# Two halves of a rational feed-forward step told apart on VectorE, with empty instructions between them

## The chip, the core and the metric

The kernel runs on one core of a Trainium2 chip. What counts is the device time of one launch in microseconds: the median of several executions. A profiled execution of the same program gives the rows quoted below.

## What is computed

For each of four batches, q, k and v of 6080 tokens by 256 channels give a channel attention (256 x 256, softmax over the last axis); its output, 24320 tokens of 256, goes through a feed-forward step of width 2048 whose activation is a rational function. Cut to what matters:

```python
qn = q / (norm(q, axis=1) + 1e-6); kn = k / (norm(k, axis=1) + 1e-6)
a = softmax(kn.transpose(0, 2, 1) @ qn / tau)      # 256 x 256 for each batch
x = (v @ a).reshape(24320, 256)
h = x @ w_in                                       # 24320 x 2048
P = a0 + a1 * h + a2 * h**2 + a3 * h**3
Q = 1 + abs(b0) * abs(h) + abs(b1) * h**2
out = (P / (Q + 1e-6)) @ w_out                     # 24320 x 256
```

## The kernel before

**Tiling.** Tokens lie on the free axis in groups of 512 (twelve a batch, the last of 448; 48 in all); the 2048 hidden channels lie on the partitions in 16 blocks of 128, taken two at a time. A *pair* is one group and two such blocks: eight pairs a group, 384 in all. Attention and w_in are fused into weights w before (`fuse`), so a pair starts with v.

**One pair** (`pair`, line 894). Its hidden values sit in `hx`, a PSUM tile of two banks, one for each block or *half* x = 0, 1; there are three such tiles. The names used below: *mm1* (TensorE, 12 matmuls, hx from vhi, vlo and w), *abs*, *zz*, *shift*, *root* and *square* (ScalarE, into d, uu and r, each over both halves), *num* (VectorE, hx from uu and hx, both halves), *one* (GpSimd, d), *quot* (VectorE, gh from hx and r, both halves), *again* (GpSimd, d times gh, by halves). Then by halves on VectorE, lines 998 to 1003: *rest* (hx of the half, less d) and *last* (gl of the half from hx and r). gh and gl are the high and low parts of the result; TensorE multiplies them with w_out into acc (*out_hi*, *out_lo*, 12 matmuls a pair). In the trace: rest is `hx<-hx,fast,d`, last is `gl<-hx,r`, num is `hx<-uu,fast,hx`, quot is `gh<-hx,fast,r`.

**Other work on VectorE.** A group ends with a transpose of acc into orow, and each next group's v is transposed into orow; sums of the scores (sacc) and low parts of w are mixed in.

**Order.** A `Planner` (line 134) gives each engine a fixed order of steps from costs and due times written by hand (`LAG`, `TIME`). Each engine then issues its instructions in that order: `InOrder` (line 73) ties every instruction to the one before it on its engine, as an order without a wait. All instructions are recorded by its line 83, so the trace shows that line for all and one goes by tiles.

**Waits.** The framework finds dependences from the tiles that instructions touch and makes a semaphore wait of each, also between two instructions of one engine. An instruction holds one wait; a further one stands in a sequencer instruction ahead of it. `apart` (line 340) declares two instructions on different halves of one hx tile as independent, if they are on different engines and share no other buffer. `half[0]` (line 495) tells it which hx tile and bank the running step uses. Two half steps on the same engine stay dependent.

**Which branch.** `body(True)` and `body(False)` are two versions of the whole program, chosen on the chip by the coefficients; with these inputs the first runs.

Of the kernel before, what the change touches and what calls it, by code (L numbers as in the profile page):

```python
# [129 lines left out]
def flat(bufs):  # L130
    return [x for b in bufs for x in (b.both if isinstance(b, Pair) else [b])]
# [165 lines left out]
def tile_channel_attention_rational_ffn(  # L297
# [37 lines left out]
    FRONT = 10  # L335

    half = [None]
    seen = {}

    def apart(eng, ins):  # L340


        if half[0] is None:
            return
        slot, bank, rest = half[0]
        for other, old, used in seen.get((slot, 1 - bank), ()):
            if other is not eng and not used & rest:
                tc.declare_no_dep(ins.ins, old.ins, reason="the two use different banks of one tile")
        mine = seen.setdefault((slot, bank), [])
        mine.append((eng, ins, rest))  # L350
        del mine[:-40]

    pe = InOrder(tc, nc.tensor, apart)
    dve = InOrder(tc, nc.vector, apart)
    act = InOrder(tc, nc.scalar, apart)
    pool = InOrder(tc, nc.gpsimd)
    sp = InOrder(tc, nc.sync)
# [16 lines left out]
    def buf(tag, shape, dtype=F32, name=None):  # L374


        def view(slot):
            sizes = dict(zip("abc", shape[1:]))
            t = homes[tag][slot]
            if t.dtype != dtype:  # L380
                t = t.bitcast(dtype)
            t = t[:, : math.prod(shape[1:])]
            names = " ".join(sizes)
            return t.rearrange(f"p ({names}) -> p {names}", **sizes) if len(sizes) > 1 else t

        homes.setdefault(tag, 0)
        homes[tag] = max(homes[tag], math.prod(shape[1:]))
        return Buf(tag, view)
# [54 lines left out]
    c0, c1, c2, l3, l2, lam, half2, kappa, eps, gain, x, y, z = (fast[:, i : i + 1] for i in range(13))  # L443
# [29 lines left out]
    def body(quick):  # L473
# [1 line left out]
        plan = planner(when)  # L475
        first = []
        II, T0 = when["pair"], when["start"]
        def step(eng, cost, key, fn, reads=(), writes=(), port=False, rank=None, ahead=None):
            new = [b for b in flat(writes) if b.tag is not None and not b.writers]
            used = {id(b): b for b in (*flat(reads), *flat(writes))}.values()  # L480
            own = [b for b in used if b.tag in ("hA", "hB")]
            rest = [b for b in used if b.tag not in ("hA", "hB")]

            def run():
                for b in new:
                    b.tile = b.view(b.slot)
                if ahead is not None:
                    where = [(b.tag, b.slot) for b in new]
                    if ahead in sent:
                        assert sent[ahead] == where  # L490
                        return
                    sent[ahead] = where
                at = {(b.slot, b.tag == "hB") for b in own}
                if len(at) == 1:
                    half[0] = *at.pop(), {(b.tag, b.slot) if b.tag else id(b) for b in rest}
                fn()
                half[0] = None

            begun = plan.add(eng, cost, key, run, reads, writes, port, rank)
            if ahead is not None:  # L500
                first.append(begun)
# [4 lines left out]
        def piece(side, m, at, c):  # L506
# [72 lines left out]
            else:  # L579
                dst, ok = None, w_out_ok[m]  # L580
                where = slice(2 * m, 2 * m + 2)
                whi, wlo = (x[:, where].rearrange("p f e -> p (f e)") for x in (w_out_hi, w_out_lo))
            step("SP", 1.45, at, load, (), [raw])
            step("ACT", 0.67, c, rescale, [raw], [kept])
            one, two = (0.45, 0.7) if port else (0.62, 0.7)
            step("POOL", 0.6, c + 0.05, sign, [kept], [kept])
            step("DVE", two, c + 0.1, top_bits, [kept], [work], port)
            step("DVE", one, c + 0.2, power, [work], [work], port)
# [305 lines left out]
        def pair(m, at, vparts, w, acc):  # L894
# [3 lines left out]
            s = n / 512  # L898
            (vhi, vlo), (whi, wlo) = vparts, w
            hx = banks()  # L900
            d, r = buf("d", [P, 2, GT]), buf("r", [P, 2, GT])
            y = buf("uu", [P, 2, GT], F32, "uu")

            def c(b):
                return b[:, :, :n]

            def due(name):
                x = lag[name]
                return at + (x[p] if isinstance(x, tuple) else x)

            def mm1(i):
                idx = 0
                for e in range(NC2):
                    for a, x in ((whi, vhi), (whi, vlo), (wlo, vhi)):
                        pe.matmul(
                            hx[:, i, :n], a[:, e, i * P : (i + 1) * P], x[:, e, :n],
                            start=(idx == 0), stop=(idx == 3 * NC2 - 1),
                        )
                        idx += 1

            for i in range(2):
                fn = lambda i=i: mm1(i)
# [8 lines left out]
                                start=(first and i == parts[0] and a is w[0]), stop=(last and i == 1 and a is w[-1]),  # L931
                            )

            def put(eng, per, fixed, name, fn, reads, writes, rank=None, later=0.0):
                step(eng, per * s + fixed, due(name) + later, fn, reads, writes, False, None if rank is None else at + rank)

            if quick:
                fn = lambda: act.activation(c(d), c(hx), AF.Abs)
                put("ACT", 0.87, 0.16, "abs", fn, [hx], [d], 1.0)
                fn = lambda: act.activation(c(y), c(hx), AF.Square, bias=half2)  # L940
                put("ACT", 0.87, 0.25, "zz", fn, [hx], [y], 1.0)
                fn = lambda: act.activation(c(d), c(d), AF.Square, bias=1.0)
                put("ACT", 0.87, 0.2, "shift", fn, [d], [d])
                fn = lambda: dve.scalar_tensor_tensor(c(hx), c(y), kappa, c(hx), op0=ALU.add, op1=ALU.mult)
                put("DVE", 1.06, 0.23, "num", fn, [y, hx], [hx])
                fn = lambda: act.activation(c(r), c(d), AF.Abs_reciprocal_sqrt, bias=eps)
                put("ACT", 0.87, 0.3, "root", fn, [d], [r], 6.0)
                fn = lambda: pool.tensor_scalar(c(d), c(d), ones[:, 0:1], eps, op0=ALU.mult, op1=ALU.add)
                put("POOL", 1.06, 0.18, "one", fn, [d], [d])
                first = c0  # L950
            else:
                kk = buf("uu", [P, 2, GT], F32, "kk")
                fn = lambda: act.activation(c(kk), c(hx), AF.Abs, scale=b1)
                put("ACT", 0.87, 0.25, "kk", fn, [hx], [kk], 1.0)
                fn = lambda: dve.scalar_tensor_tensor(c(d), c(kk), b0, c(hx), op0=ALU.add, op1=ALU.mult)
                put("DVE", 1.06, 0.22, "prod", fn, [kk, hx], [d], 1.0)
                fn = lambda: act.activation(c(d), c(d), AF.Abs)
                put("ACT", 0.87, 0.2, "absd", fn, [d], [d])
                fn = lambda: act.activation(c(y), c(hx), AF.Identity, scale=a3, bias=a2)
                put("ACT", 0.87, 0.33, "slope", fn, [hx], [y], 1.0)  # L960
                fn = lambda: dve.tensor_tensor(c(y), c(y), c(hx), op=ALU.mult)
                put("DVE", 1.06, 0.16, "num1", fn, [y, hx], [y])
                fn = lambda: dve.scalar_tensor_tensor(c(hx), c(y), a1, c(hx), op0=ALU.add, op1=ALU.mult)
                put("DVE", 1.06, 0.23, "num2", fn, [y, hx], [hx])
                fn = lambda: act.activation(c(r), c(d), AF.Abs_reciprocal_sqrt, bias=ONE)
                put("ACT", 0.87, 0.2, "root", fn, [d], [r], 6.0)
                fn = lambda: pool.tensor_scalar(c(d), c(d), ones[:, 0:1], ONE, op0=ALU.mult, op1=ALU.add)
                put("POOL", 1.06, 0.07, "one", fn, [d], [d])
                first = a0
            fn = lambda: act.activation(c(r), c(r), AF.Square)  # L970
# [3 lines left out]
            ghi, glo = buf("gh", [P, 2, GT], F32R), buf("gl", [P, 2, GT], F32R)  # L974
            ghi_ok = Buf()
            t_ok, glo_ok = ([Buf() for _ in range(2)] for _ in range(2))
            fn = lambda: dve.scalar_tensor_tensor(c(ghi), c(hx), first, c(r), op0=ALU.add, op1=ALU.mult)
# [11 lines left out]
            if AGAIN == "whole":  # L989
                fn = lambda: pool.tensor_tensor(c(d), c(d), c(ghi).bitcast(F32), op=ALU.mult)  # L990
                put("POOL", 2.32, 0.1, "again", fn, [d, ghi, ghi_ok], t_ok)

            def tail(x):
                h = hx.both[x]
                if AGAIN != "whole":
                    fn = lambda: pool.tensor_tensor(d[:, x, :n], d[:, x, :n], ghi[:, x, :n].bitcast(F32), op=ALU.mult)
                    put("POOL", 1.16, 0.145, "again", fn, [d, ghi, ghi_ok], [t_ok[x]], later=0.1 * x)
                fn = lambda: dve.scalar_tensor_tensor(
                    hx[:, x, :n], hx[:, x, :n], first, d[:, x, :n], op0=ALU.add, op1=ALU.subtract
                )  # L1000
                put("DVE", 0.53, 0.23, "rest", fn, [h, d, t_ok[x]], [h], later=0.1 * x)
                fn = lambda: dve.tensor_tensor(glo[:, x, :n], hx[:, x, :n], r[:, x, :n], op=ALU.mult)
                put("DVE", 0.53, 0.155, "last", fn, [h, r, *([glo] if x else [])], [glo_ok[x], *([] if x else [glo])], 10.0, 0.1 * x)

            for x in range(2):
                tail(x)
                out_hi(x)
                out_lo(x)
# [67 lines left out]
        for G in range(TG):  # L1076
            b, g = divmod(G, NG)
            at = T0 + G * NFP * II
# [60 lines left out]
```

## Time and profile before

| | |
|---|---|
| median of 3 runs | 2483.2 us (2482.13 to 2484.92) |
| the profiled execution | 2482.81 us, its span 2481.4 us |
| TensorE busy (granted clock 0.986 on the mean) | 2377.6 us, 96% |
| VectorE busy | 2208.8 us, 89% |
| ScalarE busy | 2061.9 us, 83% |
| GpSimd busy | 1844.5 us, 74% |

Busy means that an instruction of the engine was under way; waits of the sequencers are not in it. In a timeline row the first number is the start, the second how long the instruction took (several, where it ends in x2), and the bracket how long the engine had stood idle before it and what ended that. Two rows of one engine give the time from start to start, and so whether the second began before the first had ended.

### The profile page before, as it was taken

Reading aid. Unit: us, or ns where it says so; the run is one execution under the profiler, and the core shown is the slowest. Engines: PE = TensorE matmul, PEld = TensorE weight load, DVE = VectorE, ACT = ScalarE, POOL = GpSimd, SP = SyncE. Lnnn points to the kernel's source line nnn. Section 1 sums busy time; section 2 is a strip of 40 time slices with the busy share of each in tenths; the row PEclk is TensorE's granted clock in tenths of the full one; section 3 lists DMA queues with packets and bytes.
Section 4 is the critical chain, followed back from the end, with each engine's and each line's share of the span. In section 5 each row is a group of like instructions: output and inputs, shape, how many; then the busy total and the mean of one; then the engine's idle time right before and its main releaser. Section 6 shows DMA issues by size and latency. Waiting matters only on the chain.

```text
span 2481.4 us, 30690 instructions
## 1 busy us (share of the span) xinstructions
PE 2377.6 (96%) x10312; PEld 1926.9 (78%) x10312; DVE 2208.8 (89%) x2645; ACT 2061.9 (83%) x2052; POOL 1844.5 (74%) x1424
## 2 busy tenths in 40 slices
PE   6599999999999999999999999999999999999998
PEld 5477777887788887777778888777777877777776
DVE  4779999979978889999997889999998999999997
ACT  4589999868777789899977778899996989999896
POOL 6798777787669977777767896777774777777775
PEclk9799999999999999999999999999999999999999
DMA  8433112271246731211225661211211121111201
GB/s 261 127 104 58 18 18 35 65 145 24 43 103 133 161 58 18 34 18 18 34 59 124 128 128 25 35 18 18 34 17 18 18 33 18 25 28 18 32 11 18
DMA packets 455864, 141.17 MB, mean 57 GB/s; under 512 B 395888, under 2 KB 445040, under 8 KB 455696
## 3 DMA queue, kind: packets, MB, share of 16 engines
q1 hardware_dynamic: 447152, 108.04, 20.9%
q0 software_dynamic: 8544, 31.07, 6.9%
q8 instruction: 83, 1.36, 0.2%
q14 instruction: 85, 0.70, 0.1%
HBM read 83.10 MB, written 24.90 MB: 44 GB/s over the span
## 4 chain that ended last, share of the span: by engine, by line
PE 58%; DVE 25%; issue 9%; ACT 3%; POOL 3%; DMA 2%; DVEq 0%; SPq 0%; POOLq 0%; ACTq 0%
PE hx L83 34%; PE acc L83 24%; DVE hx L83 10%; DVE gl L83 5%; DVE gh L83 5%; DVE orow L83 2%; POOL d L83 2%; ACT d L83 1%; ACT uu L83 1%; ACT r L83 1%; DMA d<-in_moe_w_in_dram 1%; POOL orow L83 0%; POOL uu L83 0%; DVEq L83 0%; DVE kq L83 0%
## 5 line engine op out<-in xcount | busy, mean ns | idle before, releaser
L83 POOL TENSOR_TENSOR d<-d,gh 128x512 f32<-128x512 f32 (+1 forms) x768 | 977.4, 1302 | 491.4 <-DVE gh L83 478.4
L83 PE MATMUL hx<-vhi,w 128*128 128x512 f32 (+1 forms) x3072 | 1055.9, 396 | 36.5 <-DVE gl L83 30.2
L83 PEld LDWEIGHTS hx<-vhi,w 128*128 128x128 f32 x3072 | 577.4, 188 | 224.7 <-DVE gl L83 104.7
L83 DVE SCALAR_TENSOR_TENSOR hx<-hx,fast,d 128x512 f32<-128x512 f32 (+1 forms) x768 | 574.7, 748 | 80.8 <-POOL d L83 51.0
L83 PE MATMUL hx<-vlo,w 128*128 128x512 f32 (+1 forms) x1536 | 597.8, 389 | 0.0
L83 ACT ACTIVATE uu<-hx,fast 128x1024 f32<-128x1024 f32 (+1 forms) x384 | 422.6, 1100 | 173.6 <-PE hx L83 169.9
L83 DVE TENSOR_TENSOR gl<-hx,r 128x512 fp32r<-128x512 f32 (+1 forms) x768 | 521.0, 680 | 40.2 <-PE acc L83 4.0
L83 DVE SCALAR_TENSOR_TENSOR hx<-uu,fast,hx 128x1024 f32<-128x1024 f32 (+1 forms) x384 | 487.1, 1268 | 36.2 <-ACT d L83 19.2
L83 POOL TENSOR_SCALAR d<-d,ones,fast 128x1024 f32<-128x1024 f32 (+1 forms) x384 | 467.9, 1218 | 68.8 <-ACT r L83 65.8
L83 DVE SCALAR_TENSOR_TENSOR gh<-hx,fast,r 128x1024 fp32r<-128x1024 f32 (+1 forms) x384 | 484.5, 1262 | 32.6 <-ACT r L83 26.8
L83 PE MATMUL acc<-gh,w_out_hi 128*128 128x512 f32 (+1 forms) x1536 | 476.9, 392 | 1.9 <-DVE sacc L83 0.9
L83 ACT ACTIVATE d<-hx 128x1024 f32<-128x1024 f32 (+1 forms) x384 | 387.6, 1009 | 109.0 <-PE hx L83 89.2
L83 PE MATMUL acc<-gl,w_out_hi 128*128 128x512 f32 (+1 forms) x1536 | 475.2, 391 | 2.7 <-DVE gl L83 2.4
L83 PE MATMUL acc<-gh,w_out_lo 128*128 128x512 f32 (+1 forms) x1536 | 472.0, 389 | 0.0
L83 ACT ACTIVATE r<-d,fast 128x1024 f32<-128x1024 f32 (+1 forms) x384 | 439.3, 1144 | 11.9
L83 ACT ACTIVATE r<-r 128x1024 f32<-128x1024 f32 (+1 forms) x384 | 403.2, 1050 | 8.9
L83 ACT ACTIVATE d<-d 128x1024 f32<-128x1024 f32 (+1 forms) x384 | 403.7, 1051 | 7.5
L83 PEld LDWEIGHTS acc<-gl,w_out_hi 128*128 128x128 f32 x1536 | 288.4, 188 | 62.5 <-DVE gl L83 5.5
L83 PEld LDWEIGHTS acc<-gh,w_out_hi 128*128 128x128 f32 x1536 | 288.9, 189 | 60.5 <-DVE orow L83 2.3
L83 PEld LDWEIGHTS acc<-gh,w_out_lo 128*128 128x128 f32 x1536 | 289.5, 189 | 58.0
L83 PEld LDWEIGHTS hx<-vlo,w 128*128 128x128 f32 x1536 | 289.3, 188 | 47.6
L83 PE MATMUL hx<-kq 128*128 128x256 f32 (+1 forms) x592 | 135.8, 384 | 8.3 <-DVE fast L83 7.5
(111 smaller groups left out, 1147.1 us busy)
## 6 DMA issues: line engine op xcount, KB each, us to landing
ssq<-sq POOLq DMA_DIRECT2D x54, 512.0 KB, 4.9
vst<-in_v_dram SPq DMA_DIRECT2D x176, 128.0 KB, 4.0
out_dram<-orow SPq DMA_DIRECT2D x176, 128.0 KB, 3.3
kq<-in_k_dram SPq DMA_DIRECT2D x78, 256.0 KB, 4.3
kq<-in_q_dram SPq DMA_DIRECT2D x78, 256.0 KB, 4.6
d<-in_moe_w_in_dram SPq DMA_DIRECT2D x8, 512.0 KB, 6.6
ssq<-sq POOLq DMA_DIRECT2D x6, 448.0 KB, 5.4
d<-in_moe_w_out_dram SPq DMA_DIRECT2D x4, 512.0 KB, 3.8
```

What stands on the lines that cost most here:

```text
L83: ins = op(*args, **kwargs)
```

## The change

`apart` gets a fourth entry, a *lane*: (pair, half) for the steps rest and last of the branch-independent tail, none for all others. Two instructions whose lanes name the same pair and different halves are now declared independent also on the same engine, and without the test for shared buffers. Where a step with a lane comes right behind a step of the same engine with the same pair and the other half, an empty instruction (`dve.nop()`) is issued between the two; it goes through `InOrder` as well, so the order runs through it. The planner's input is the same.

```diff
@@ -335,19 +335,20 @@
     FRONT = 10
 
     half = [None]
-    seen = {}
+    seen, recent = {}, {}
 
     def apart(eng, ins):
 
 
         if half[0] is None:
             return
-        slot, bank, rest = half[0]
-        for other, old, used in seen.get((slot, 1 - bank), ()):
-            if other is not eng and not used & rest:
+        slot, bank, rest, lane = half[0]
+        for other, old, used, side in seen.get((slot, 1 - bank), ()):
+            beside = lane is not None and side is not None and lane[0] == side[0] and lane[1] != side[1]
+            if beside or (other is not eng and not used & rest):
                 tc.declare_no_dep(ins.ins, old.ins, reason="the two use different banks of one tile")
         mine = seen.setdefault((slot, bank), [])
-        mine.append((eng, ins, rest))
+        mine.append((eng, ins, rest, lane))
         del mine[:-40]
 
     pe = InOrder(tc, nc.tensor, apart)
@@ -475,7 +476,7 @@
         plan = planner(when)
         first = []
         II, T0 = when["pair"], when["start"]
-        def step(eng, cost, key, fn, reads=(), writes=(), port=False, rank=None, ahead=None):
+        def step(eng, cost, key, fn, reads=(), writes=(), port=False, rank=None, ahead=None, lane=None):
             new = [b for b in flat(writes) if b.tag is not None and not b.writers]
             used = {id(b): b for b in (*flat(reads), *flat(writes))}.values()
             own = [b for b in used if b.tag in ("hA", "hB")]
@@ -490,9 +491,13 @@
                         assert sent[ahead] == where
                         return
                     sent[ahead] = where
+                old = recent.get(eng)
+                if lane is not None and old is not None and old[0] == lane[0] and old[1] != lane[1]:
+                    dve.nop()
+                recent[eng] = lane
                 at = {(b.slot, b.tag == "hB") for b in own}
                 if len(at) == 1:
-                    half[0] = *at.pop(), {(b.tag, b.slot) if b.tag else id(b) for b in rest}
+                    half[0] = *at.pop(), {(b.tag, b.slot) if b.tag else id(b) for b in rest}, lane
                 fn()
                 half[0] = None
 
@@ -931,8 +936,8 @@
                                 start=(first and i == parts[0] and a is w[0]), stop=(last and i == 1 and a is w[-1]),
                             )
 
-            def put(eng, per, fixed, name, fn, reads, writes, rank=None, later=0.0):
-                step(eng, per * s + fixed, due(name) + later, fn, reads, writes, False, None if rank is None else at + rank)
+            def put(eng, per, fixed, name, fn, reads, writes, rank=None, later=0.0, lane=None):
+                step(eng, per * s + fixed, due(name) + later, fn, reads, writes, False, None if rank is None else at + rank, lane=lane)
 
             if quick:
                 fn = lambda: act.activation(c(d), c(hx), AF.Abs)
@@ -998,9 +1003,9 @@
                 fn = lambda: dve.scalar_tensor_tensor(
                     hx[:, x, :n], hx[:, x, :n], first, d[:, x, :n], op0=ALU.add, op1=ALU.subtract
                 )
-                put("DVE", 0.53, 0.23, "rest", fn, [h, d, t_ok[x]], [h], later=0.1 * x)
+                put("DVE", 0.53, 0.23, "rest", fn, [h, d, t_ok[x]], [h], later=0.1 * x, lane=(m, x))
                 fn = lambda: dve.tensor_tensor(glo[:, x, :n], hx[:, x, :n], r[:, x, :n], op=ALU.mult)
-                put("DVE", 0.53, 0.155, "last", fn, [h, r, *([glo] if x else [])], [glo_ok[x], *([] if x else [glo])], 10.0, 0.1 * x)
+                put("DVE", 0.53, 0.155, "last", fn, [h, r, *([glo] if x else [])], [glo_ok[x], *([] if x else [glo])], 10.0, 0.1 * x, (m, x))
 
             for x in range(2):
                 tail(x)
```

## Rows read from the trace of the kernel before

**Rows 1.** The page's part 1: busy us (share of span) xinstructions

```profile
PE 2377.6 (96%) x10312; PEld 1926.9 (78%) x10312; DVE 2208.8 (89%) x2645; ACT 2061.9 (83%) x2052; POOL 1844.5 (74%) x1424
```

**Rows 2.** Waits, longest first: who waited for whom: us in total, times, longest

```profile
PEld hx L83 <- DVE gl L83: 107.9, 215, 3.0
...
DVE hx L83 <- POOL d L83: 51.0, 120, 4.1
PE hx L83 <- DVE gl L83: 31.2, 48, 2.6
```

**Rows 3.** The page's part 4: the chain that ended last, by engine

```profile
PE 58%; DVE 25%; issue 9%; ACT 3%; POOL 3%; DMA 2%; DVEq 0%; SPq 0%; POOLq 0%; ACTq 0%
```

**Rows 4.** Timeline of VectorE, 1200 to 1216 us, one undisturbed pair

```profile
1204.18 1.28 DVE L83 SCALAR_TENSOR_TENSOR hx<-uu,fast,hx 128x1024 f32<-128x1024 f32 x1
1205.37 0.75 DVE L83 SCALAR_TENSOR_TENSOR hx<-hx,fast,d 128x512 f32<-128x512 f32 x1
1206.23 0.69 DVE L83 TENSOR_TENSOR gl<-hx,r 128x512 fp32r<-128x512 f32 x1
1207.02 0.76 DVE L83 SCALAR_TENSOR_TENSOR hx<-hx,fast,d 128x512 f32<-128x512 f32 x1
...
1209.48 1.28 DVE L83 SCALAR_TENSOR_TENSOR hx<-uu,fast,hx 128x1024 f32<-128x1024 f32 x1
```

**Rows 5.** The chain that ended last, whole span: start us, us, what

```profile
426.35 4.38 PE hx L83 x18
...
901.60 2.73 PE hx L83 x12
1004.91 4.42 PE hx L83 x18
...
1095.98 4.38 PE hx L83 x18
...
1114.90 2.72 PE acc L83 x12
...
2171.38 4.38 PE hx L83 x18
```

**Rows 6.** Timeline of ScalarE, 1204 to 1211 us

```profile
1204.59 1.06 ACT L83 ACTIVATE r<-r 128x1024 f32<-128x1024 f32 x1
1206.02 1.03 ACT L83 ACTIVATE d<-hx 128x1024 f32<-128x1024 f32 x1 [0.37 <-PE hx L83]
...
1210.22 1.06 ACT L83 ACTIVATE r<-r 128x1024 f32<-128x1024 f32 x1
```

**Rows 7.** Timeline of VectorE, 1126 to 1142 us, around two transposes

```profile
1132.69 1.27 DVE L83 SCALAR_TENSOR_TENSOR gh<-hx,fast,r 128x1024 fp32r<-128x1024 f32 x1
1133.89 0.68 DVE L83 TENSOR_TENSOR gl<-hx,r 128x512 fp32r<-128x512 f32 x1
...
1135.67 1.24 DVE L83 STREAM_TRANSPOSE orow<-acc 128x1024 f32<-128x1024 f32 x1
1136.84 1.20 DVE L83 STREAM_TRANSPOSE orow<-vst 128x1024 f32<-128x1024 f32 x1
...
1139.13 1.61 DVE L83 SCALAR_TENSOR_TENSOR hx<-hx,fast,d 128x512 f32<-128x512 f32 x2
1140.77 0.69 DVE L83 TENSOR_TENSOR gl<-hx,r 128x512 fp32r<-128x512 f32 x1
1141.38 0.75 DVE L83 SCALAR_TENSOR_TENSOR hx<-hx,fast,d 128x512 f32<-128x512 f32 x1
```

**Rows 8.** The chain that ended last, 1126 to 1142 us

```profile
1131.96 0.02 DVEq L83
...
1132.93 0.02 DVEq L83
```

**Rows 9.** Timeline of TensorE matmuls, 1140 to 1142.2 us

```profile
1140.37 0.61 PE L83 MATMUL acc<-gh,w_out_lo 128*128 128x512 f32 x2
1141.52 0.50 PE L83 MATMUL hx<-vhi,w 128*128 128x512 f32 x1 [0.54 <-DVE gl L83]
```

## What it does to the time

> **What bounds the kernel now.** I read the page's busy shares first: TensorE is busy for 2377.6 us of the 2481.4 us span, VectorE for 89% [rows 1]. So a faster VectorE can only pay where TensorE stands still for it. The list of waits says who holds TensorE up: its weight loads and matmuls for hx wait longest for VectorE's gl, 107.9 and 31.2 us [rows 2]. A weight load runs ahead of the matmuls, so not all of that is lost; measured as matmul starts later than 227 ns after the one before (203 ns for the short groups), counting gaps over 60 ns and leaving out the first 115 us, TensorE loses 113 us, 60 us of them (146 stops) released by gl. The chain that ended last agrees: 58% of the span on PE, 25% on DVE [rows 3]. The stops come because mm1 of a pair writes a bank of hx that "last", three pairs earlier, still reads.
>
> Now the rate of each engine in an undisturbed pair. VectorE: from one num (1204.18) to the next (1209.48) 5.30 us [rows 4]. TensorE: 12 matmuls take 2.72 us [rows 5], so 24 take 5.44. ScalarE: from one Square of r (1204.59) to the next (1210.22) 5.63 us, 0.37 of it waiting for PE, so 5.26 of its own [rows 6]. TensorE is slowest, and VectorE follows 0.14 us behind. But each group of eight pairs also has two transposes on VectorE, 1.24 and 1.20 us [rows 7]: 8 x 5.30 + 2.44 - 0.2 (overlaps) = 44.6 us against TensorE's 43.5. VectorE falls behind once a group and TensorE stops. That is the place where the change can pay.
>
> **What the change removes.** Two VectorE instructions with nothing between them start 0.09 us before the earlier one ends: num at 1204.18 takes 1.28, the rest behind it starts at 1205.37. Where the later one waits for the earlier, there is a hole instead: last at 1206.23 takes 0.69, the next rest starts at 1207.02, 0.10 behind its end [rows 4]. In the chain such a hole shows VectorE's sequencer for 0.02 us, as at 1131.96 [rows 8]. Both orders are in the trace for the pair last, then rest: of the same pair 0.79 us from start to start [rows 4], of another pair 0.61 (1140.77 to 1141.38) [rows 7]. So one removed wait is worth 0.18 us.
>
> I went through VectorE's timeline from end to end, beside the order of its instructions in the program, and counted neighbours of one pair and different halves:
> - last of half 0, then rest of half 1: 214 times, holes of 0.10; worth 0.186 on the mean.
> - rest of half 0, then rest of half 1: 100 times; 64 with a hole of 0.10, worth 0.194; 36 that stand still for GpSimd's product anyway, worth nothing.
> - rest of half 1, then last of half 0: 141 times; 75 with 0.10 (0.194), 64 with 0.03 (0.12), such as 1139.13 + 1.61 to 1140.77 [rows 7]. Last of half 0 must still wait for rest of half 0, but that is then one instruction further back. Other waits that far back leave no hole: the gl at 1133.89 has one, for the rest before the gh. Its sequencer piece lies at 1132.93, under that gh (1132.69, 1.27 us), and it starts 0.07 us before the gh ends [rows 7, 8].
> - rest, then last of the same half (258 times) is a true dependence and stays.
>
> That is 39.8 + 12.4 + 22.2 = 74 us of VectorE's time, or 0.19 us a pair. In the undisturbed stretches it buys nothing: VectorE would need 5.11 us a pair and TensorE 5.44.
>
> **What it adds.** An empty instruction wherever the half changes between neighbours of a pair: the 455 above, and 22 times between last and last, where no wait stands today. No empty instruction is in this trace. The lower bound is 0: sequencer pieces whose condition is met lie under the running instruction, as at 1132.93 [rows 8]. Upper bound: that it holds the queue until the earlier instruction is done, which is today's hole, and adds an exposed step of its own. Such a step is the difference between holes with a sequencer piece and without, 0.10 - 0.03 = 0.07 us [rows 7, 8]. I take 0, as the met condition is the nearest row: the empty instruction waits for nothing. Behind it on VectorE is only the half step that it orders. The order of work, the queues of SP and GpSimd and all DMAs are untouched.
>
> The Trainium skill bears on the empty instruction too (PSUM — Partial Sum Buffer, "Engine vs sequencer instructions"): it is of the sequencer, which waits for earlier instructions only to be dispatched. By that its price is 0; no run shows it yet.
>
> **What reaches the end.** A chain made shorter bounds the gain from above: the other chains may come last, never sooner. On the chain that ended last lie 60 of the first kind (11.2 us), 44 of the second (8.5), 44 of the third with the short hole (5.5) and 18 with the long one (3.5): **28.7 us at most**.
>
> Where they lie says how much of it is real. (a) 16 times the chain leaves TensorE, runs 14.1 us through VectorE over the two transposes and returns to a matmul for hx; first at 426.35, last at 2171.38 [rows 5]. In the one at 1141.52 three removed holes lie (at 1131.96, inside the 1.61 of two rests at 1139.13, before 1140.77) [rows 7, 8]: 0.19 + 0.19 + 0.12 = 0.50 us. The matmul that ends it starts at 1141.52, where the two before it began at 1140.37 and 1140.60 [rows 9], so without a stop it would be at 1140.83: 0.69 us lost, more than is saved. All 0.50 are taken: 16 x 0.50 = **8.0 us**. (b) 21 other stretches hold 20.7 us; the longest runs through VectorE and GpSimd from 904.3 (901.60 + 2.73) to 1004.91 [rows 5] with 20 holes, 3.6 us. There TensorE stops many times (3.9 us in that one), and GpSimd hands over on the chain, where the holes don't count. If each stretch gives back only what the stop at its end costs, it is 11.1 us; if all, 20.7. No row is nearer to either end; I take the middle, 15.9.
>
> 8.0 + 15.9 = 23.9 us, between 19 and 28.7. The profiled execution took 2482.81 us, 1.4 outside its span, 0.4 under the median of 2483.2: 2482.8 - 23.9 = 2458.9, with the 0.4 **2459 us**.
>
> **Rivals.**
> (B) *Another engine is next late.* ScalarE needs 5.26 us of the 5.44 and GpSimd's d is the last thing some rests wait for (51.0 us in 120 waits [rows 2, 6]). When VectorE comes 0.2 us sooner those become its waits, and the long stretches of (b) give little: 8 us and less than 11, so 5 to 19 us, some 2471. For it: the GpSimd hand-overs on those stretches. Against: the removed holes don't lie between gh and the rest that waits for GpSimd, so GpSimd gets its input sooner as well.
> (C) *No change, 2483.* The later half waits in hardware for the earlier one although no semaphore says so, or the empty instruction keeps that wait. The mechanism would show here as a hole of at least 0 behind every instruction; the overlaps of 0.09 and the last-then-rest of 0.61 us [rows 4, 7] speak against it.
> This is what the Trainium skill says (VectorE: DVE Perf Modes, "The DRAIN you can't avoid"): the next instruction starts only when the pipe is empty, waits between chained instructions cost nothing extra, and they can't be saved by leaving out semaphores. By that rule the sum is 0 and the time 2483. The trace disagrees with it for these shapes, by 0.18 us for one wait [rows 4, 7].
> (D) *Slower.* The empty instruction stops the queue until its forerunner is done, and then costs its own 0.07 us: holes of 0.17 where 0.10 stood, 0.07 x 122 + 0.14 x 44 = 14.7 us on the chain with the same holes, some 2497. It decides from a price over 0.19 us for one. Against: sequencer pieces with a met condition are hidden [rows 8].
>
> **How the numbers follow.** Forecast (gain 19 to 28.7): 0.62. B: 0.18. C: 0.13. D: 0.05. More than the chain allows, as the instructions themselves change: 0.02. What a measurement can tell from no change is about 0.2%, 5 us: faster 0.62 + 0.18 + 0.02 = 0.82, same 0.13, slower 0.05. The range takes the forecast and B: 2483.2 - 28.7 less 1.5 of scatter, 2453, to 2478.
>
> **What would show it.** Right: rest of half 1 starts some 0.08 us before its forerunner's end; a 14.1 us stretch shrinks to 13.6 with a stop of 0.2; the groups come 45.0 us apart instead of 45.5 (1095.98 to 1141.52 [rows 5, 9]); waits of TensorE for gl fall by a fifth or more; VectorE's steady pairs show idle time before rest, released by GpSimd. Wrong: holes of 0.10 still there (C), wider ones (D), or the holes gone and the groups still 45.5 us apart (B at its worst). The sum is wrong too if the order of the instructions is not that of before.

## The result, and the profile after

The changed kernel takes **2420.7 us** (median of 4 runs, 2419.4 to 2423.1) against 2482.7 of the kernel before in the same comparison: 0.9753 [0.9736, 0.977], 62 us or 2.5% less. The profiled execution took 2419.42 us, its span is 2418.0, so 63.4 us less than the span before. The forecast was 2459 with a range from 2453: the direction was right, the gain is two and a half times as large, and the time lies outside the range.

Busy time by engine of the profile after, to be held against [rows 1], and below it the shares of the chain that ended last, against [rows 3]:

```profile
PE 2339.0 (97%) x10312; PEld 1939.2 (80%) x10312; DVE 2173.7 (90%) x2645; ACT 2058.7 (85%) x2052; POOL 1845.6 (76%) x1424
```

```profile
PE 82%; DVE 8%; ACT 4%; issue 3%; DMA 2%; POOL 1%; SPq 0%; DVEq 0%; POOLq 0%
```

TensorE is busy 39 us less with the same matmuls, as stops that the records don't show as idle have gone (told below, with the step that failed), and the chain runs along it still more. Every engine runs as many instructions as before, and in the trace the sequence of operations and tiles is the same on every engine. No row tells of an empty instruction, and the program built from the changed kernel holds none: it ordered the work while the program was made. What went is on VectorE's sequencer: 275 semaphore instructions fewer (1598 to 1323), the ones that held a second wait.

Waits after, against [rows 2] (us in total, times, longest):

```profile
DVE hx L83 <- POOL d L83: 51.0, 117, 4.2
...
PEld hx L83 <- DVE gl L83: 29.4, 51, 2.9
...
PE hx L83 <- DVE gl L83: 13.1, 12, 2.5
```

TensorE's weight loads wait 29 us for gl where they waited 108, its matmuls 13 where they waited 31; VectorE waits for GpSimd as long as before.

Timeline of VectorE after, from the transposes that end one group to those of the next; it answers [rows 4] and [rows 7]:

```profile
1065.29 1.24 DVE L83 STREAM_TRANSPOSE orow<-acc 128x1024 f32<-128x1024 f32 x1
...
1068.74 1.40 DVE L83 SCALAR_TENSOR_TENSOR hx<-hx,fast,d 128x512 f32<-128x512 f32 x2
1070.05 0.68 DVE L83 TENSOR_TENSOR gl<-hx,r 128x512 fp32r<-128x512 f32 x1
...
1087.31 1.28 DVE L83 SCALAR_TENSOR_TENSOR hx<-uu,fast,hx 128x1024 f32<-128x1024 f32 x1
1088.50 0.75 DVE L83 SCALAR_TENSOR_TENSOR hx<-hx,fast,d 128x512 f32<-128x512 f32 x1
1089.35 0.69 DVE L83 TENSOR_TENSOR gl<-hx,r 128x512 fp32r<-128x512 f32 x1
1089.96 0.75 DVE L83 SCALAR_TENSOR_TENSOR hx<-hx,fast,d 128x512 f32<-128x512 f32 x1
...
1092.41 1.28 DVE L83 SCALAR_TENSOR_TENSOR hx<-uu,fast,hx 128x1024 f32<-128x1024 f32 x1
...
1109.08 1.24 DVE L83 STREAM_TRANSPOSE orow<-acc 128x1024 f32<-128x1024 f32 x1
```

The holes behind the half steps have become overlaps. From last (1089.35) to the next rest (1089.96) it is 0.61 us where it was 0.79 [rows 4]; two rests end to end take 1.40 instead of 1.61 [rows 7]; the last at 1070.05 starts before the rests are done. The hole that stays, 1088.50 + 0.75 to 1089.35, is the true dependence of last on rest in one half. A pair takes 5.10 us (1087.31 to 1092.41) instead of 5.30, and a group, from one transpose of acc to the next, 43.79 us (1065.29 to 1109.08) instead of 45.53, from this row of the kernel before to the one at 1135.67 [rows 7]:

```profile
1090.14 1.24 DVE L83 STREAM_TRANSPOSE orow<-acc 128x1024 f32<-128x1024 f32 x1
```

Those transposes close each group, so their starts split the span. Of the 47 groups so bounded, 27 take 45.5 to 45.9 us before and have no attention work in them; call these *regular*. They add up to 1230.6 us before and 1182.9 after, 47.7 less, with medians of 45.54 and 43.80. The other 20 add up to 1050.1 and 1038.2, 11.9 less. They are of two kinds: twelve in which VectorE also works for the attention gave 3.5 us together, eight without such work (at the start, at the short end of a batch, one behind the attention) gave 8.3. The stretch ahead of the first transpose is 3.7 us shorter (191.3 and 187.6), which may be scatter: it lay between 186 and 191 in all runs that keep this order. The end is equal. 47.7 + 11.9 + 3.7 = 63.3.

So the question is why a regular group gives 1.74 us (1.77 on the mean), where the chain held only 0.50.

### The profile page after: what moved, and what is told of

Read it like the earlier page. It is cut to its first block, busy times and chain, and to the rows that moved or that the text cites. A ratio compares the mean times of both kernels' runs of the same rounds, so it can differ in the third digit from the quotient of the medians.

```text
span 2418.0 us, 30415 instructions
## 1 busy us (share of the span) xinstructions
PE 2339.0 (97%) x10312; PEld 1939.2 (80%) x10312; DVE 2173.7 (90%) x2645; ACT 2058.7 (85%) x2052; POOL 1845.6 (76%) x1424
## 3 DMA queue, kind: packets, MB, share of 16 engines
q8 instruction: 83, 1.36, 0.2%
## 4 chain that ended last, share of the span: by engine, by line
PE 82%; DVE 8%; ACT 4%; issue 3%; DMA 2%; POOL 1%; SPq 0%; DVEq 0%; POOLq 0%
PE hx L83 45%; PE acc L83 37%; DVE hx L83 3%; ACT d L83 1%; DVE gh L83 1%; DVE gl L83 1%; ACT uu L83 1%; ACT r L83 1%; DVE orow L83 1%; DMA kq<-in_q_dram 1%; POOL d L83 1%; DMA d<-in_moe_w_in_dram 1%; DVE kq L83 0%; POOL uu L83 0%; DVE y L83 0%
## 5 line engine op out<-in xcount | busy, mean ns | idle before, releaser
L83 PE MATMUL hx<-vhi,w 128*128 128x512 f32 (+1 forms) x3072 | 1035.3, 391 | 15.5 <-DVE gl L83 13.1
L83 DVE SCALAR_TENSOR_TENSOR hx<-hx,fast,d 128x512 f32<-128x512 f32 (+1 forms) x768 | 566.6, 745 | 51.7 <-POOL d L83 51.0
L83 ACT ACTIVATE r<-d,fast 128x1024 f32<-128x1024 f32 (+1 forms) x384 | 439.5, 1145 | 11.9
```

Of the source, the lines that this page charges most:

```text
L83: ins = op(*args, **kwargs)
```

## The experiments

**Two theories.** *Chain*: a group is as long as the chain that the profile infers. The stretch that goes through VectorE takes 14.1 of its 45.5 us and has three removed holes on it; the rest belongs to TensorE, and holes under it give nothing. *Budget*: VectorE sets the length of the regular groups from end to end, and every hole counts. The reason for the second is a view that the prediction does not use: VectorE's groups of instructions between two transposes of the kernel before (busy us, mean ns of one | idle us ahead of them, and for whom).

```profile
L83 DVE SCALAR_TENSOR_TENSOR hx<-hx,fast,d 128x512 f32<-128x512 f32 x16 | 12.1, 754 | 1.5 <-POOL d L83 0.9
L83 DVE SCALAR_TENSOR_TENSOR hx<-uu,fast,hx 128x1024 f32<-128x1024 f32 x9 | 11.5, 1277 | 0.0
L83 DVE TENSOR_TENSOR gl<-hx,r 128x512 fp32r<-128x512 f32 x16 | 11.0, 686 | 0.9
L83 DVE SCALAR_TENSOR_TENSOR gh<-hx,fast,r 128x1024 fp32r<-128x1024 f32 x8 | 10.2, 1270 | 0.0
```

The last column is the point. In a whole group VectorE stands still 2.4 us: 0.9 for GpSimd (three waits of 0.28 us), never for TensorE or ScalarE, and the other 1.5 in holes of its own. An engine that hardly waits for any other is likely to be the bound of its stretch; the runs below test it. The same view after the change:

```profile
L83 DVE SCALAR_TENSOR_TENSOR hx<-hx,fast,d 128x512 f32<-128x512 f32 x16 | 11.9, 751 | 0.8 <-POOL d L83 0.8
...
L83 DVE TENSOR_TENSOR gl<-hx,r 128x512 fp32r<-128x512 f32 x16 | 10.9, 684 | 0.6
```

1.5 of the idle column became 0.8, and 0.9 became 0.6. Nine holes a group have gone; of the tenth removed wait nothing is gained, because that rest stands still for GpSimd anyway. The nine gave 1.66 us in the group that begins at 1090.14, eight of them 0.19 and one 0.14, and with instructions that start some 0.1 us sooner in all it is the 1.74.

### The holes of two parts of the pairs

The lanes are kept for some pairs of a group only; in all others the old waits are back. First pairs 4 and 5, and all but these:

```diff
-lane=(m, x))
+lane=(m, x) if p in (4, 5) else None)
```

> The changed kernel with the lane (and so the independence) kept for the fifth and sixth pair of a group alone: in a group without attention work this removes exactly the three holes that the forecast found on the chain, some 0.50 us. Theory A, the forecast's (TensorE holds such a group for 31.4 of its 45.5 us, VectorE only for the 14.1 us stretch): the group goes from 45.5 to 45.0. Theory B (VectorE alone sets such a group with all its instructions, holes and waits): the same 45.0. Total by both 2465 to 2471 us.

> The reverse: the lane kept for the six other pairs alone. Seven of the ten holes of a group without attention work go, none of them on the chain as the forecast read it. Theory A: such a group stays at 45.5 us, since its stretch of 14.1 us is as long as before; total about 2475. Theory B: every hole counts wherever it lies, 7 x 0.17 = 1.2 us, the group takes 44.3; 27 such groups and some of the others, total about 2443.

My split missed its aim: the pair numbers were off by four. Pairs 4 and 5 hold two holes between last and rest, neither on the chain; the three chain holes lie in pairs 0 and 1, next to the transposes. Read so, the runs still speak. Pairs 4 and 5 alone: 2468.7 us, 0.9956 [0.994, 0.9973]. All others: 2434.2 us, 0.9816 [0.98, 0.9832]. VectorE's timeline, first of the former, then of the latter:

```profile
1125.78 1.24 DVE L83 STREAM_TRANSPOSE orow<-acc 128x1024 f32<-128x1024 f32 x1
...
1170.94 1.25 DVE L83 STREAM_TRANSPOSE orow<-acc 128x1024 f32<-128x1024 f32 x1
```

```profile
1114.49 1.24 DVE L83 STREAM_TRANSPOSE orow<-acc 128x1024 f32<-128x1024 f32 x1
...
1158.69 1.25 DVE L83 STREAM_TRANSPOSE orow<-acc 128x1024 f32<-128x1024 f32 x1
```

A group of 45.16 us instead of 45.54 is 0.39 less for two holes that the chain says are free; 44.20 is 1.34 less for the other seven. That is 0.19 a hole in both. (The total of 2443 that was expected of the second by the budget was 9 us too high; the group's 44.3 was met.)

I then aimed again: pairs 0 and 1 (the three chain holes), and pairs 2 to 7 (the six off the chain).

```diff
-lane=(m, x))
+lane=(m, x) if p in (0, 1) else None)
```

> The pairs of the two runs before were counted wrong by four: the three holes that the forecast found on the chain lie in the first and second pair of a group, not in the fifth and sixth. Here the lane is kept for the first and second pair alone, so that exactly these three holes go. Theory A (chain): 0.50 us a group, 45.0. Theory B (all of VectorE's time counts): also 0.50 to 0.55, 45.0; total about 2465. It is the counterpart of the next one.

> The lane kept for the other six pairs alone: the six removable holes of a group without attention work that are not on the chain as the forecast read it. Theory A: such a group stays at 45.5 us, total about 2475. Theory B: 6 x 0.19 = 1.14 us less, 44.4; total about 2443.

Pairs 0 and 1: 2462.5 us, 0.9922 [0.9906, 0.9939]. Pairs 2 to 7: 2440.2 us, 0.9831 [0.9815, 0.9848]. Their transposes of acc, in that order:

```profile
1123.53 1.24 DVE L83 STREAM_TRANSPOSE orow<-acc 128x1024 f32<-128x1024 f32 x1
...
1168.52 1.25 DVE L83 STREAM_TRANSPOSE orow<-acc 128x1024 f32<-128x1024 f32 x1
```

```profile
1117.05 1.24 DVE L83 STREAM_TRANSPOSE orow<-acc 128x1024 f32<-128x1024 f32 x1
...
1161.42 1.25 DVE L83 STREAM_TRANSPOSE orow<-acc 128x1024 f32<-128x1024 f32 x1
```

The six holes off the chain shorten a group to 44.37, by 1.19; the three on it by 0.54 (medians of all regular groups: 44.35 and 45.00). By the chain theory the six give nothing. They give more than twice what the chain holes give, and the two runs add up to the whole: 0.54 + 1.19 = 1.73 us a group of 1.74, and 19.5 + 41.7 = 61 us of 62. For the regular groups the chain theory is false.

### Work taken from TensorE

If VectorE sets the group, less work on TensorE must leave it as long as it is, before the change and after it. mm1 drops two of its 12 matmuls (one execution of each kernel):

```diff
-for a, x in ((whi, vhi), (whi, vlo), (wlo, vhi)):
+for a, x in ((whi, vhi), (whi, vlo), (wlo, vhi))[: 3 - e]:
```

> The kernel before with the product of w's low part and v's high part left out for the second half of the channels: 10 matmuls for hx in place of 12, 0.45 us less of TensorE in each pair, 3.6 us in a group; nothing else changes. Theory A: the part of the group that the chain has on TensorE shrinks in proportion, 3.6 x 31.4 / 45.5 = 2.5 us, to about 43.0. Theory B: VectorE sets the group, it stays at 45.5, and only the groups with attention work, where TensorE is full, get shorter.

> The changed kernel with the same two matmuls of each pair left out. If the changed kernel's groups of 43.8 us are now held by TensorE (192 matmuls at 0.227 us are 43.5), they go to about 40 to 42. If VectorE still sets them (theory B in full), they stay at 43.8.

On the kernel before, 2461.9 us. One regular group of it in VectorE's timeline, then its chain by engine, then its waits for gl:

```profile
1076.49 1.24 DVE L83 STREAM_TRANSPOSE orow<-acc 128x1024 f32<-128x1024 f32 x1
...
1122.04 1.24 DVE L83 STREAM_TRANSPOSE orow<-acc 128x1024 f32<-128x1024 f32 x1
```

```profile
DVE 46%; PE 19%; issue 15%; POOL 9%; ACT 8%; DMA 2%; DVEq 1%; SPq 0%; POOLq 0%; ACTq 0%
```

```profile
PEld hx L83 <- DVE gl L83: 250.4, 432, 3.3
...
PE hx L83 <- DVE gl L83: 79.2, 184, 3.0
```

A twelfth of TensorE's work in these groups is gone, 3.6 of 43.5 us, and a group takes 45.55 as before; the 27 add up to 1231.0. What TensorE saves it spends waiting for gl. With that much slack on TensorE the chain says what was true already: DVE 46%, PE 19%. Of the 21 us by which its span is shorter, 18 lie in the other 20 groups (1050.1 to 1032.1), all of them in the twelve named above, and 3 ahead of the first transpose, within the scatter told above.

The same cut on the changed kernel: 2396.2 us. Its transposes of acc:

```profile
1052.81 1.24 DVE L83 STREAM_TRANSPOSE orow<-acc 128x1024 f32<-128x1024 f32 x1
...
1096.62 1.24 DVE L83 STREAM_TRANSPOSE orow<-acc 128x1024 f32<-128x1024 f32 x1
```

43.81 a group, as in the changed kernel uncut; the 27 add up to 1183.1. So VectorE sets the regular groups after the change too, and with TensorE out of the way the change is worth the same 47.9 us there (1231.0 - 1183.1).

### The empty instruction left out

The lanes stay, the empty instructions go:

```diff
-                old = recent.get(eng)
-                if lane is not None and old is not None and old[0] == lane[0] and old[1] != lane[1]:
-                    dve.nop()
-                recent[eng] = lane
```

> The changed kernel without the empty instructions: the half steps are as independent, but nothing ties the second of two neighbours of a pair to the first, and the framework then moves many of VectorE's instructions to other places (the other engines keep their order). If the order is what the empty instruction is for, this loses a good part of the 62 us, perhaps all; if the planned order doesn't matter much, it stays near 2421.

2519.5 us, 1.0148 [1.0131, 1.0165]: slower than the kernel before, and 99 us slower than the change. The declaration of independence removes the order along with the wait, and VectorE's instructions come in another sequence (other tiles at 513 of 2645 places; the other engines keep theirs). Its timeline and its longest waits:

```profile
1202.97 0.76 DVE L83 SCALAR_TENSOR_TENSOR hx<-hx,fast,d 128x512 f32<-128x512 f32 x1
1204.00 0.76 DVE L83 SCALAR_TENSOR_TENSOR hx<-hx,fast,d 128x512 f32<-128x512 f32 x1 [0.28 <-POOL d L83]
1204.67 0.68 DVE L83 TENSOR_TENSOR gl<-hx,r 128x512 fp32r<-128x512 f32 x1
1205.27 1.27 DVE L83 SCALAR_TENSOR_TENSOR gh<-hx,fast,r 128x1024 fp32r<-128x1024 f32 x1
1206.46 0.68 DVE L83 TENSOR_TENSOR gl<-hx,r 128x512 fp32r<-128x512 f32 x1
```

```profile
DVE hx L83 <- POOL d L83: 180.5, 317, 7.2
...
PEld hx L83 <- DVE gl L83: 111.6, 127, 6.6
...
PE hx L83 <- DVE gl L83: 65.6, 82, 6.2
```

The second rest now stands ahead of the first last and waits for GpSimd's product with nothing done in between: 180.5 us of such waits in 317 instances, against 51.0 in 117. Both lasts come later, one of them behind gh, and TensorE waits for them again. Regular groups take 45.1 us, the other 20 add up to 1094.0. So the loss is not there: regular groups are still 0.4 us shorter than before the change, but the other 20 are 44 us longer and the first transpose comes 10 us later. The worth of the empty instruction is that it holds the order; a cost of its own shows nowhere, as the holes of the changed kernel are gone with it in place.

### How much is left on VectorE

On the changed kernel, from the tenth group on half of each transpose of v is left out, so VectorE has half a microsecond less in a group (the source side is cut likewise):

```diff
-turned[:, :, :n].rearrange("p e (k j) -> p k e j", j=32),
+turned[:, :, :n].rearrange("p e (k j) -> p k e j", j=32)[:, : K // 2 if G > 8 else K],
```

> The changed kernel with half of each transpose of v left out from the tenth group on: some 0.6 us less of VectorE in a group. VectorE sets the groups of 43.8 us (theory B); TensorE needs 192 x 0.2267 = 43.5. So such a group goes down by about 0.25 us, to TensorE's 43.55, and not by 0.6. That is what is left to be had from VectorE in these groups.

2414.6 us (one execution). Its two transposes, and the one that ends the group:

```profile
1108.35 1.24 DVE L83 STREAM_TRANSPOSE orow<-acc 128x1024 f32<-128x1024 f32 x1
1109.51 0.67 DVE L83 STREAM_TRANSPOSE orow<-vst 128x512 f32<-128x512 f32 x1
...
1151.88 1.25 DVE L83 STREAM_TRANSPOSE orow<-acc 128x1024 f32<-128x1024 f32 x1
```

The transpose takes 0.67 us instead of 1.20, 0.53 less, but the group shrinks only from 43.80 to 43.53. That is TensorE's 43.5 (8 x 5.44), and in this group none of its matmuls starts later than 0.227 us behind the one before: after 0.27 us the bound changes hands. VectorE's regular groups have 27 x 0.27 = some 7 us more to give, 0.3%.

## Why the prediction was wrong

**Right.** The holes: behind every freed half step the overlap is 0.08 to 0.09 us, on all 214 of the first kind. Their price: 0.18 forecast, 0.19 a hole measured in the runs with part of the pairs. The unchanged order, and that order is what could have gone wrong (the run without the empty instruction shows by how much). Rivals C and D are out: no freed hole stayed, none grew. With C falls, for these instructions, the rule of the Trainium skill (VectorE: DVE Perf Modes, "The DRAIN you can't avoid") that a semaphore wait between chained instructions costs nothing extra: it is 0.79 us from start to start with the wait and 0.61 without it, and the 455 waits between instructions of one engine were worth 2.5% of the time. The same section of the Trainium skill adds that a next instruction which isn't held starts earlier, which the prediction left out; the overlaps of 0.08 to 0.09 us agree with that.

**Right by luck.** The price of the empty instruction is 0, but not for the reason given. The prediction argued that a sequencer instruction with a met condition is hidden under the running one. No such instruction is in the program or the trace, so what one costs on the chip stays unmeasured.

**The step that failed** is "What reaches the end": "A chain made shorter bounds the gain from above", with "16 x 0.50" and "28.7 us at most" that follow from it. A true critical path does bound the gain so. The chain of a profile is inferred, and here it was not that path: the run with pairs 2 to 7 took holes out of the regular groups that were not on it there, and these groups alone gave 32.9 us (1230.6 to 1197.7). In the place of 16 x 0.50 = 8.0 us stand 27 groups with 1.77 on the mean, 47.7 us. Only 0.02 of the chances was given to more than the chain allows, and that for another reason, that the instructions themselves change.

Why the chain stays on TensorE can be read in the trace of before. One stop in four views, each with its own fence: VectorE's timeline, that of TensorE's weight loads, that of its matmuls, and the chain:

```profile
1105.62 0.69 DVE L83 TENSOR_TENSOR gl<-hx,r 128x512 fp32r<-128x512 f32 x1
```

```profile
1106.37 0.19 PEld L83 LDWEIGHTS hx<-vhi,w 128*128 128x128 f32 x1 [0.44 <-DVE gl L83]
```

```profile
1105.97 0.90 PE L83 MATMUL hx<-vhi,w 128*128 128x512 f32 x2
1106.71 0.39 PE L83 MATMUL hx<-vlo,w 128*128 128x512 f32 x1
1106.94 0.62 PE L83 MATMUL hx<-vhi,w 128*128 128x512 f32 x2
```

```profile
1104.96 1.39 PE hx L83 x6
1106.36 0.01 issue
1106.37 1.66 PE hx L83 x6
```

gl ends at 1106.31, and the weight load that waited for it starts at 1106.37. TensorE has stood still meanwhile: the row of two matmuls at 1105.97 is 0.90 us long where the next such row is 0.62, its second one starts at 1106.37, 0.40 behind the first instead of 0.227, and the six that begin there take 1.66 us on the chain where six at full pace take 1.36. A matmul's modelled end, though, lies 0.39 us behind its start. A stop of up to some 0.16 us (0.39 - 0.227) is covered by the end of the matmul before, so no idle time shows; here 0.01 of issue is all that is left, and the chain goes on along PE instead of crossing to VectorE. In the regular group around this row TensorE stops four times, each 0.05 to 0.06 us behind the end of a gl, and loses 1.71 us by it; in the group of the changed kernel from 1065.29 it does so once and loses 0.17. The longest of the four, ahead of 1095.98, is the only one that the chain crossed at, as it did in the next group ahead of 1141.52. The 113 us of TensorE's losses that the prediction had measured fell to some 60, so the loss was in the text; it was capped by the chain instead of being followed.

**"In the undisturbed stretches it buys nothing"** was wrong for the same reason. I compared rates in one pair, 5.30 of VectorE with 5.44 of TensorE, and left the two transposes to the place where they stand. Their 2.4 us are a debt that VectorE works off over all eight pairs, at 0.14 a pair, and can't (8 x 0.14 = 1.1): TensorE waits for it at several places of the group, and a faster pair anywhere pays the debt sooner. The prediction had the sum that says so, 8 x 5.30 + 2.44 - 0.2 = 44.6 us against 43.5. With the 0.86 us that VectorE waits for GpSimd in a group it is 45.5, the length of the group itself. From there the answer is one subtraction: nine holes less, 45.5 - 1.65 = 43.85, still above TensorE's 43.5, so all of it counts, 27 x 1.65 = 44.6 us, and a forecast of some 2438 before anything from the other groups.

**Term (b)**, 15.9 us from the other stretches, was nearer: the 20 other groups gave 11.9. That is in part luck, since 8.3 of it came from the eight in which VectorE has no attention work. In the twelve in which it has, which gave 3.5, rival B's outcome holds: the holes are gone, but some of these groups stay as long as they were (49.85 and 49.87, 56.71 and 56.81 for two of them), and VectorE's waits for GpSimd stay at 51.0 us in the whole. What sets these groups was not tried one by one; that TensorE's work has a share is shown by the two runs with two matmuls fewer, where the cut took 19.5 us off the twelve before the change and 18.5 after it. B's own mechanism, ScalarE or GpSimd next late, is not shown.

**The signs** that I had named were met beyond their size: groups 43.8 apart instead of 45.0, waits for gl down by 70% (weight loads and matmuls together, 139.1 to 42.5) instead of a fifth. The idle time before rest that was to show in steady pairs didn't grow, because VectorE is still the later engine.

## What to carry to other kernels

Take the longest stretch that repeats, write up every engine's budget over the whole of it, and look for the engine whose idle time names no other engine (or only short waits): that one is likely to set the time, whatever the chain shows, and then each microsecond off it counts until the next budget is reached. A chain that runs along TensorE can hide short stops, as it did here, so let it not cap a gain; taking work from TensorE in a run tells at once whether it is the bound. Where independence is declared to be rid of a wait, give the order something else to stand on, since without it the gain of 62 us became a loss of 38.

## What the runs showed of the hardware

After a stop for a weight load, TensorE's second matmul starts late as well: at 1106.71 behind 1106.37 it is 0.34 us, where the pace is 0.227. The 0.11 us came behind all 128 stops of the kernel before in which a matmul of 512 columns began right behind the end of a gl, and behind all 32 of the kernel after. The stop of 0.17 us at 1106.37 so costs 0.29.

A semaphore wait for an instruction of the same engine costs 0.19 us between two VectorE instructions of 0.7 us, and 0.12 where the awaited one is already further back. An empty instruction of the framework that only carries the order left no row in the trace and no time; it was gone before the chip.
